# Reordering the first 60 microseconds of a fused spectral filter and max-of-two layer

## The chip, the core and the metric

One core of a Trainium2 chip runs one program. The core has five engines that run independently, each through its own queue of instructions in order: TensorE (PE in the profile, with its weight loads as PEld), VectorE (DVE), ScalarE (ACT), GpSimd (POOL) and SyncE (SP, which here only issues DMAs). An instruction waits for the semaphores of what it needs, and everything behind it on the same queue waits too. The metric is the device time of one execution in microseconds (us); lower is better. The kernel before takes 503.54 us (median of 3 runs, 503.17 to 504.83).

## What is computed

The input x has 8 batches of 3072 positions and 256 channels. Each batch is transformed with a real FFT along the positions, multiplied by a complex filter, and transformed back. The result goes through a small layer with two hidden products of width 1024 whose larger value is kept, and an output product.

```python
X = np.fft.rfft(x, axis=1)
F = (filt_r + 1j * filt_i)[None, :, :]
y = np.fft.irfft(X * F, n=x.shape[1], axis=1)
x = y.reshape(B * S, D)
g = np.maximum(x @ w1, x @ w2)
out = g @ w_out
```

## The kernel before

The FFT of length 3072 = 96 x 32 is done as matrix products in stages, in bf16: a 96-point transform (f1 for batch 1, s1 for later batches, L317 to L356), a trip through DRAM that regroups the result (written from `at` to `ad`, read back as `bt`, f1_read at L334 and s1_read at L358), a 32-point transform (s2, L371), the product with the filter, the inverse 32-point transform (s3, L392), another trip through DRAM (zd to zr, z_read), and the inverse 96-point transform s4 (L422), which leaves a tile of 384 positions in `yt`, channels on the partitions.

The layer uses max(a, b) = relu(a - b) + b. So the kernel holds Wd = w1 - w2, the output weights Wo, and M = w2 Wo, and computes out = relu(y Wd) Wo + y M. Wd is formed on POOL by `prep_wd` (L290), from the f32 copies of w1 and w2 in the buffer WS, which SP's DMAs fill (load_w, L279). w2 is cast to bf16 by DVE in four pieces (`cast_w2`, L284), turned by PE and copied by ACT in two halves (`prep_t`, L294), and multiplied with Wo (`prep_m`, L302). Wo itself comes in by one DMA on POOL's queue, with a cast from f32 (`load_wo`, L287).

The work of the layer is cut into 64 tiles of 384 positions, eight for each batch. Tile tt takes eight steps j of the main loop (L693 to L709). In step j, `moe_h` (L442) makes one 128-wide slice of the hidden products of tile tt (two matmuls, `ph`) and lets DVE or ACT apply the relu; `moe_o` (L463) makes three or four of the 30 matmuls (`po`) that give the output of tile tt - 1: three blocks c of 128 positions, each a sum of eight products with Wo and two with M. Two blocks share one PSUM tile, which DVE copies to `ot` before two DMAs on POOL's queue write it out. In tile 0 the two products with M come last in each block.

The order on every engine is the order of the calls: nothing is rescheduled. `plan(b, step, fn, ...)` (L656) hangs other work behind a step; a batch has 64 steps. In batch 0 these are the rest of `t2` (batch 0's last regrouping), the casts and `prep_t` and `prep_m`, batch 1's f1 in 16 pieces c (plan_f1, L659: each piece one PE matmul and one copy, on ACT for even c and on DVE for odd c; after each odd c SP writes the pair to `ad`), and then f1_read, which issues two DMAs that fill bt for batch 1, 12 columns u each. `plan_f2` (L666) hangs the visits of batch 1 (s2, product, s3, and s1 for batch 2) into fixed steps, the first at step 24, and on SP's queue the loads `load_xf` of batch 2's x (four DMAs for each of the first three pieces, L90 to L98), folded on POOL by `fold` (L100).

Ahead of the main loop stands the opening, which loads x and the filter, makes the tables, and takes batch 0 through its transform. POOL ends it with products of the filter (L382 and L389), then the loads of batch 1's x (`load_x(1, c, 2)`, L88: two of its eight chunks each; chunk k feeds f1 pieces 2k and 2k + 1), prep_wd, load_wo and the table CT. `spin` (L556) issues matmuls whose results nobody uses.

DMA issues carry a lane as well: each of the two families of queues (SP's, POOL's) reuses eight semaphores in turn, so that a DMA also waits until the one eight places before it has landed.

Of the kernel before, what the change touches and what calls it, by code (L numbers as in the profile page):

```python
# [8 lines left out]
FP32 = mybir.dt.float32  # L9
# [6 lines left out]
D = 256  # L16
# [10 lines left out]
def kernel(  # L27
# [15 lines left out]
    V, S, G, TE = nc.vector, nc.scalar, nc.gpsimd, nc.tensor  # L43
# [25 lines left out]
    pso = ctx.enter_context(tc.tile_pool(name="pso", bufs=2, space=bass.MemoryType.PSUM))  # L69
# [8 lines left out]
    def x_tile(b, c):  # L78
        if c % 2 == 0:
            xb[b] = xpool.tile([128, 8, D], BF16, tag="xb", name="xb")  # L80
        return xb[b][:, 4 * (c % 2):4 * (c % 2) + 4]

    def load_x(b, c, n):
        for k in range(c, c + n):
            xb[b, k] = x_tile(b, k)[0:NP]
        src = x[b].rearrange("(p m) d -> p m d", m=NM)
        m0 = 4 * (c % 2)
        G.dma_start(out=xb[b][0:NP, m0:m0 + 4 * n], in_=src[:, 4 * c:4 * c + 4 * n, :])  # L88
# [98 lines left out]
    def table_ct():  # L187
        G.memset(CT, 0.0)
        for g in range(2):
            G.tensor_copy(CT[64 * g:64 * g + 48, :, 0:48].rearrange("p s (u r) -> p s u r", r=2),  # L190
                          C1[0:48].rearrange("p (u s r) -> p s u r", s=2, r=2))
# [92 lines left out]
    def cast_w2(h, c):  # L284
        V.tensor_copy(w2b[:, c, 512 * h:512 * h + 512], w2f[:, c, 512 * h:512 * h + 512])

    def load_wo():  # L287
        G.dma_start(out=Wo, in_=moe_w_out.rearrange("(c p) j -> p c j", p=128))

    def prep_wd(h, engine):  # L290
        js = slice(512 * h, 512 * h + 512)
        engine.tensor_tensor(Wd[:, :, js], w1f[:, :, js], w2f[:, :, js], OP.subtract)  # L292

    def prep_t(jp):  # L294
# [127 lines left out]
    def s4(tt):  # L422
        b, i = divmod(tt, 8)
        y_ = ypool.tile([128, 2, 384], BF16, tag="yt", name="y_")
        for dc in range(2):
            py = ps.tile([128, 4, NP], FP32, tag="ps", name="py")
            for m in range(4):
                TE.matmul(py[:, m], zr[b][:, 4 * i + m, 128 * dc:128 * dc + 128], G1, start=True, stop=True)  # L428
            o_ = y_[:, dc].rearrange("p (t m) -> p t m", m=4)
            i_ = py.rearrange("p m t -> p t m")  # L430
            if dc == 0:
                S.activation(o_, i_, AF.Copy, scale=1.0 / 1536.0)
            else:
                V.tensor_scalar(o_, i_, 1.0 / 1536.0, None, OP.mult)
        yt[tt] = y_
# [18 lines left out]
    po = {}  # L454
    ot = {}

    def out_block(tt, c):
        b, i = divmod(tt, 8)
        dst = out[b * N:(b + 1) * N].rearrange("(c p i m) d -> c i p (m d)", c=3, p=32, i=8)[c, i]
        E = G if tt < 8 * B - 2 else nc.sync  # L460
        E.dma_start(out=dst, in_=ot[tt // 2][:, 3 * (tt % 2) + c])  # L461

    def moe_o(tt, k0, k1):  # L463
        y_, g_ = yt[tt], gt[tt]
        for k in range(k0, k1):
            c, e = divmod(k, 10)
            n = (e + 2) % 10 if tt == 0 else e
            q = 3 * tt + c
            blk = slice(128 * c, 128 * c + 128)
            if e == 0 and (q % 2 == 0 or q == 24 * B - 1):  # L470
                po[0] = pso.tile([128, 2, D], FP32, tag="po", name="po")
            p_ = po[0][:, q % 2]
            if n < 2:
                TE.matmul(p_, y_[:, n, blk], M[:, n], start=(e == 0), stop=(e == 9))  # L474
            else:
                TE.matmul(p_, g_[:, n - 2, blk], Wo[:, n - 2], start=(e == 0), stop=(e == 9))  # L476
            if e == 9 and q >= 24 * B - 2:
                e = q % 6
                if q % 2 == 0:
                    S.activation(ot[tt // 2][:, e], p_, AF.Copy)  # L480
                else:
                    V.tensor_copy(ot[tt // 2][:, e], p_)
                out_block(tt, c)
            elif e == 9 and q % 2 == 1:
                if q % 6 == 1:
                    ot[tt // 2] = opool.tile([128, 6, D], FP32, tag="ot", name="ot")
                e = q % 6
                V.tensor_copy(ot[tt // 2][:, e - 1:e + 1], po[0])  # L488
                for qq in (q - 1, q):
                    out_block(qq // 3, qq % 3)  # L490

# [26 lines left out]
    def s3t(v, pq):  # L518
        pool, tag = (ps, "ps") if v % 2 else (pso, "po")
        pz = [pool.tile([128, 2, 2, 2, 2, NM], FP32, tag=tag, name="pt%d" % g) for g in range(2)]  # L520
        for _ in range(2 if v == 1 else 1):
            TE.matmul(pz[0].rearrange("p i s r c m -> p (i s r c m)"), W1[:, 0:128], W1, start=True, stop=True)
        for i in range(2):
            for s in range(2):
                for dc in range(2):
                    for q, tab in enumerate((VP, VQ)):
                        for g in range(2):
                            TE.matmul(pz[g][:, i, s, :, dc], pq[s][64 * g:64 * g + 64, q, i, 128 * dc:128 * dc + 128],  # L528
                                      tab[64 * g:64 * g + 64, 2 * v + i, s].rearrange("p (r m) -> p r m", r=2),
                                      start=(q == 0), stop=(q == 1))  # L530
        zv = zT.rearrange("p c m (w g) q -> p w g (c m) q", g=2)
        for g in range(2):
            o_ = zv[:, 2 * v:2 * v + 2, g]
            i_ = pz[g].rearrange("p i s r c m -> p i (c m) (s r)")
            if v >= 4 and g == 1:
                V.tensor_copy(o_, i_)
            else:
                S.activation(o_, i_, AF.Copy)

    def t2(c, engines):  # L540
        if c == 0:
            zr[0] = zrpool.tile([96, NM, D], BF16, tag="zr", name="zr")
        n = 4 // len(engines)
        for k, engine in enumerate(engines):
            pr = ps.tile([96, n, D], BF16, tag="ps", name="pr")
            m0 = 4 * c + n * k
            for m in range(n):
                for dc in range(2):
                    TE.transpose(pr[:, m, 128 * dc:128 * dc + 128], zT[:, dc, m0 + m].rearrange("p u q -> p (u q)"),  # L549
                                 I128)  # L550
            if engine is V:
                V.tensor_copy(zr[0][:, m0:m0 + n], pr)  # L552
            else:
                S.activation(zr[0][:, m0:m0 + n], pr, AF.Copy)

    def spin(n):  # L556
        for _ in range(n):
            pd = ps.tile([128, 512], FP32, tag="ps", name="pd")
            TE.matmul(pd, W1[:, 0:128], W1, start=True, stop=True)  # L559
# [70 lines left out]
        pqs[v] = products(v)  # L630
    for v in (4, 5):
        s3t(v, pqs[v])
    for c in (2, 4):
        load_x(1, c, 2)
    prep_wd(0, G)
    load_wo()
    load_x(1, 6, 2)
    prep_wd(1, G)
    table_ct()
    setup.close()  # L640
    apool = ctx.enter_context(tc.tile_pool(name="apool", bufs=3))
# [4 lines left out]
    f1(1, 0, S)  # L646
    spin(1)
    t2(0, (V, S))
    spin(2)
    s4(0)  # L650
    spin(2)


# [2 lines left out]
    def plan(b, step, fn, *a):  # L656
        todo.setdefault((b + step // 64, step % 64), []).append((fn, a))

    def plan_f1(b, nb, steps, read):  # L659
        for c, n in zip(range(1, 16), steps):  # L660
            plan(b, n, f1, nb, c, S if c % 2 == 0 else V)
        plan(b, read, f1_read, nb)
# [12 lines left out]
            plan(b, steps[-1] + (6 if b else 11), s1_read, b + 2)  # L675

    plan(0, 2, t2, 1, (V,))
    for h in range(2):
        for c in range(2):
            plan(0, 3 + 2 * h + c, cast_w2, h, c)  # L680
    plan(0, 5, prep_t, 0)
    plan(0, 7, prep_t, 1)
    plan(0, 8, prep_m)
    for c in range(2, 8):
        plan(0, 8 * (c - 2) + 8, t2, c, (V,))
    plan_f1(0, 1, (0, 1, 1, 3, 4, 4, 5, 6, 6, 7, 8, 10, 11, 11, 12), 13)
    plan_f2(0, (24, 28, 31, 35, 38, 42, 46), ((0,), (1,), (2,), (3,), (4,), (5,), (6, 7)),
            (6, 10, 14, 18, 21, 25, 29, 33), (14, 18, 21, 25, 28, 32, 36, 40))
    for b in range(1, B - 1):
        plan_f2(b, (7, 14, 18, 24, 31, 38, 42) if b > 1 else (14, 18, 24, 30, 34, 39, 42), ((0, 1), (2,), (3,), (4,), (5,), (6,), (7,)),  # L690
                range(-32, 32, 8) if b > 1 else range(-25, 31, 7), range(-22, 42, 8) if b > 1 else range(-15, 41, 7))
# [1 line left out]
    for tt in range(8 * B + 1):  # L693
        b, i = divmod(tt, 8)
        k = 0
        for j in range(8):
# [5 lines left out]
            if tt > 0:  # L702
                n = 3 if j in (3, 7) else 4
# [36 lines left out]
```

## Time and profile before

The profiled execution of the kernel before took 503.8 us, of which 502.0 us lie between its first and last instruction.

| what | value |
|---|---|
| median of 3 runs | 503.54 us (503.17 to 504.83) |
| profiled execution, its span | 503.8 us, 502.0 us |
| PE busy | 488.4 us (97%) |
| DVE, ACT, POOL busy | 331.9, 308.3, 257.5 us |
| granted TensorE clock, mean | 0.992 |
| DMA traffic | 97.20 MB, 194 GB/s |
| PE idle in us 34 to 46 | 2.04 us of 12 |
| PE idle in us 46 to 56 | 0.18 us of 10 |

Busy is the time in which an engine has at least one instruction in work; matmuls overlap, so a busy PE is not necessarily a full one. "A <- B" in a list of waits means that engine and line A stood idle until B was done. A DMA has a time of issue on its queue and a time to landing, from the issue to the last byte's semaphore.

### The profile page before, as it was taken

The page shows a single profiled execution, that of the slowest core. Times are in us where ns is not written, and L with a number is a line of the kernel's source. Part 1 is how long each engine was busy: PE and PEld are TensorE (multiplying, and loading weights), DVE is VectorE, ACT ScalarE, POOL GpSimd, SP SyncE. Part 2 cuts the span into 40 slices and gives each one's busy share as a digit, 9 for nine tenths or more (in the row PEclk, how much of TensorE's full clock was granted, in tenths as well). Part 3 has the DMA queues.
Part 4 walks back from the last instruction along what each step waited for, and adds up shares of the span by engine and source line. Part 5 has one row for each costly group of instructions (what it writes and reads, how often), then busy time and mean ns, then how long its engine had stood idle before and what let it go on. Part 6 is the DMA issues. An engine that isn't in the chain of part 4 may idle for free.

```text
span 502.0 us, 13079 instructions
## 1 busy us (share of the span) xinstructions
PE 488.4 (97%) x5299; PEld 362.1 (72%) x5303; DVE 331.9 (66%) x518; ACT 308.3 (61%) x629; POOL 257.5 (51%) x338
## 2 busy tenths in 40 slices
PE   8688999999999999999999999999999999999997
PEld 3455777777777777777777777777777777777775
DVE  7876688457865777457765687557765687555553
ACT  6776478647774676557764586647774465544442
POOL 7893569547463864645654855537632221222220
PEclk9989999999999999999999999999999999999999
DMA  7999789995799667986779558896769235411112
GB/s 125 150 252 217 230 229 290 306 274 171 212 268 260 175 204 234 250 229 189 198 244 275 187 177 245 235 239 197 197 181 255 78 111 153 168 65 64 64 64 84
DMA packets 77966, 97.20 MB, mean 194 GB/s; under 512 B 8017, under 2 KB 54354, under 8 KB 77842
## 3 DMA queue, kind: packets, MB, share of 16 engines
q1 hardware_dynamic: 64642, 66.73, 49.6%
q0 software_dynamic: 13264, 29.64, 20.3%
q8 instruction: 41, 0.67, 0.6%
q14 instruction: 19, 0.16, 0.1%
HBM read 53.87 MB, written 47.19 MB: 201 GB/s over the span
## 4 chain that ended last, share of the span: by engine, by line
PE 90%; DMA 5%; POOL 2%; issue 1%; ACT 1%; DVE 0%; SPq 0%; POOLq 0%; DVEq 0%
PE po L476 34%; PE ph L448 33%; PE po L474 8%; PE pz L399 5%; PE py L428 4%; PE pa L349 2%; DMA F<-in_filt_r_dram 2%; PE px L376 2%; DMA Wo<-in_moe_w_out_dram 2%; POOL xb L88 1%; DMA F<-F 1%; PE pr L549 1%; POOL pq L382 0%; PE pt L528 0%; PE pm__1132 L306 0%
## 5 line engine op out<-in xcount | busy, mean ns | idle before, releaser
L476 PE MATMUL po<-Wo,gt 128*128 128x256 bf16 x1536 | 261.0, 273 | 0.2 <-DMA Wo<-in_moe_w_out_dram 0.2
L452 ACT ACTIVATE gt<-ph 128x384 bf16<-128x384 f32 x321 | 157.0, 496 | 147.9 <-PE ph L448 147.3
L461 POOL DMA_DIRECT2D out_dram<-ot x186 | 102.6, 555 | 187.1 <-DVE ot L488 184.4
L476 PEld LDWEIGHTS <-gt 128*128 128x128 bf16 x1536 | 146.6, 98 | 66.1 <-issue 10.3
L450 DVE TENSOR_SCALAR gt<-ph 128x384 bf16<-128x384 f32 x191 | 104.9, 552 | 63.1 <-PE ph L448 59.9
L382 DVE TENSOR_TENSOR pq<-px,F 128x1024 bf16<-128x1024 f32 x91 | 107.0, 1219 | 24.2 <-PE px L376 22.6
L448 PEld LDWEIGHTS <-Wd 128*128 128x128 bf16 x1024 | 96.5, 98 | 12.9 <-POOL Wd L292 1.4
L103 POOL TENSOR_TENSOR xb<-XF 128x512 bf16<-128x512 f32 x48 | 61.2, 1276 | 41.3 <-DMA XF<-in_x_dram 21.2
L488 DVE COPY ot<-po 128x512 f32<-128x512 f32 x95 | 65.1, 685 | 25.3 <-PE po L476 25.0
L104 POOL TENSOR_TENSOR xb<-XF 128x512 bf16<-128x512 f32 x48 | 61.0, 1271 | 0.0
L403 ACT ACTIVATE zt<-pz 128x512 bf16<-128x512 f32 x84 | 45.6, 595 | 11.5 <-PE pz L399 8.4
L353 ACT ACTIVATE at<-pa 128x512 bf16<-128x512 f32 x96 | 51.8, 610 | 1.2 <-PE pa L349 0.8
L428 PE MATMUL py<-G,zr 96*128 96x96 bf16 x512 | 32.7, 206 | 0.2
L428 PEld LDWEIGHTS <-zr 96*128 96x128 bf16 x512 | 29.0, 97 | 2.5 <-DVE zr L552 0.4
L399 PE MATMUL pz<-pq,VP 64*64 64x256 bf16 x336 | 21.9, 281 | 0.0
L376 PE MATMUL px<-bt,U 64*64 64x256 bf16 x384 | 19.8, 278 | 1.2 <-ACT VQ L273 0.7
L399 PE MATMUL pz<-pq,VQ 64*64 64x256 bf16 x336 | 20.9, 269 | 0.0
L349 PE MATMUL pa<-xb,CT 64*64 64x512 bf16 x192 | 19.5, 383 | 0.0
L399 PEld LDWEIGHTS <-VP 64*64 64x64 bf16 x336 | 9.7, 105 | 13.3 <-issue 13.3
L376 PEld LDWEIGHTS <-U 64*64 64x64 bf16 x384 | 10.4, 109 | 3.9 <-issue 3.3
L559 PE MATMUL pd<-W 128*128 128x512 bf16 x30 | 10.5, 462 | 1.7 <-DVE zero L145 1.5
L552 DVE COPY zr<-pr 96x1024 bf16<-96x1024 bf16 (+1 forms) x8 | 5.2, 649 | 8.0 <-PE pr L549 8.0
(429 smaller groups left out, 609.7 us busy)
## 6 DMA issues: line engine op xcount, KB each, us to landing
out_dram<-ot POOLq DMA_DIRECT2D x186, 128.0 KB, 3.3
XF<-in_x_dram SPq DMA_DIRECT2D x96, 192.0 KB, 4.6
ad<-at SPq DMA_DIRECT2D x56, 192.0 KB, 3.3
bt<-ad SPq DMA_DIRECT2D x14, 768.0 KB, 9.1
zd<-zt SPq DMA_DIRECT2D x42, 256.0 KB, 2.7
zr<-zd SPq DMA_DIRECT2D x56, 192.0 KB, 4.8
WS<-in_moe_w_dram SPq DMA_DIRECT2D x4, 512.0 KB, 5.1
xb<-in_x_dram POOLq DMA_DIRECT2D x8, 192.0 KB, 5.8
```

Source lines behind the costliest of these rows:

```text
L103: G.tensor_tensor(t_[:, 0], f[:, 0], f[:, 1], OP.add)
L104: G.tensor_tensor(t_[:, 1], f[:, 0], f[:, 1], OP.subtract)
L353: S.activation(at[:, m0:m0 + 2], pa[g], AF.Copy)
L382: E.tensor_tensor(pq, px.rearrange("p (o i) d -> p o i d", o=1).to_broadcast([128, 2, 2, D]), F[:, :, 2 * v:2 * v + 2, s], OP.mult)
L399: TE.matmul(pz[g][64 * s:64 * s + 64, i], tab[64 * g:64 * g + 64, 2 * v + i, s], pq[s][64 * g:64 * g + 64, q, i], start=(q == 0), stop=(q ...
L428: TE.matmul(py[:, m], zr[b][:, 4 * i + m, 128 * dc:128 * dc + 128], G1, start=True, stop=True)
L448: TE.matmul(ph, Wd[:, dc, 128 * j:128 * j + 128], y_[:, dc], start=(dc == 0), stop=(dc == 1))
L450: V.tensor_scalar(gt[tt][:, j], ph, 0.0, None, OP.max)
L452: S.activation(gt[tt][:, j], ph, AF.Relu)
L461: E.dma_start(out=dst, in_=ot[tt // 2][:, 3 * (tt % 2) + c])
L476: TE.matmul(p_, g_[:, n - 2, blk], Wo[:, n - 2], start=(e == 0), stop=(e == 9))
L488: V.tensor_copy(ot[tt // 2][:, e - 1:e + 1], po[0])
```

## The change

On POOL's queue at the end of the opening, the order is now: load of x chunks 2 and 3, W_out, three quarters of w1 - w2, the loads of x chunks 4 to 7, the last quarter of w1 - w2. Before, it was: x chunks 2 to 5, the first half of w1 - w2, W_out, x chunks 6 and 7, the second half. `prep_wd` takes quarters (256 of the 1024 columns) in place of halves.

On DVE, two of the four casts of w2 move into the opening, around s4(0); the other two hang behind steps 4 and 5 (before: the four behind steps 3 to 6). `prep_t(0)` moves from step 5 to step 3 and `prep_m` from step 8 to step 9.

Tile 0's blocks are done in another order, FIRST: the Wo products of blocks 0 and 2, then the M products of both, then block 1. Blocks 0 and 2 lie in different PSUM tiles, so `po` now holds two.

Batch 1's f1 pieces 8 and up move from steps 6 to 12 to steps 9 to 13, piece 4 from step 3 to 2, piece 6 from 4 to 5 and piece 7 from 5 to 6; f1_read moves from step 13 to 14. The first two loads of batch 2's x move from steps 6 and 10 to steps 10 and 12. Nothing is added or taken out but the split of two POOL instructions into four.

```diff
--- before.py
+++ after.py
@@ -287,8 +287,8 @@
     def load_wo():
         G.dma_start(out=Wo, in_=moe_w_out.rearrange("(c p) j -> p c j", p=128))
 
-    def prep_wd(h, engine):
-        js = slice(512 * h, 512 * h + 512)
+    def prep_wd(q, engine):
+        js = slice(256 * q, 256 * q + 256)
         engine.tensor_tensor(Wd[:, :, js], w1f[:, :, js], w2f[:, :, js], OP.subtract)
 
     def prep_t(jp):
@@ -460,16 +460,20 @@
         E = G if tt < 8 * B - 2 else nc.sync
         E.dma_start(out=dst, in_=ot[tt // 2][:, 3 * (tt % 2) + c])
 
+
+    FIRST = ([(c, e) for c in (0, 2) for e in range(8)] + [(c, e) for c in (0, 2) for e in (8, 9)]
+             + [(1, e) for e in range(10)])
+
     def moe_o(tt, k0, k1):
         y_, g_ = yt[tt], gt[tt]
         for k in range(k0, k1):
-            c, e = divmod(k, 10)
-            n = (e + 2) % 10 if tt == 0 else e
+            c, e = divmod(k, 10) if tt else FIRST[k]
+            n = e if tt else (e + 2) % 10
             q = 3 * tt + c
             blk = slice(128 * c, 128 * c + 128)
             if e == 0 and (q % 2 == 0 or q == 24 * B - 1):
-                po[0] = pso.tile([128, 2, D], FP32, tag="po", name="po")
-            p_ = po[0][:, q % 2]
+                po[q // 2 % 2] = pso.tile([128, 2, D], FP32, tag="po", name="po")
+            p_ = po[q // 2 % 2][:, q % 2]
             if n < 2:
                 TE.matmul(p_, y_[:, n, blk], M[:, n], start=(e == 0), stop=(e == 9))
             else:
@@ -485,7 +489,7 @@
                 if q % 6 == 1:
                     ot[tt // 2] = opool.tile([128, 6, D], FP32, tag="ot", name="ot")
                 e = q % 6
-                V.tensor_copy(ot[tt // 2][:, e - 1:e + 1], po[0])
+                V.tensor_copy(ot[tt // 2][:, e - 1:e + 1], po[q // 2 % 2])
                 for qq in (q - 1, q):
                     out_block(qq // 3, qq % 3)
 
@@ -630,12 +634,13 @@
         pqs[v] = products(v)
     for v in (4, 5):
         s3t(v, pqs[v])
-    for c in (2, 4):
+    load_x(1, 2, 2)
+    load_wo()
+    for q in range(3):
+        prep_wd(q, G)
+    for c in (4, 6):
         load_x(1, c, 2)
-    prep_wd(0, G)
-    load_wo()
-    load_x(1, 6, 2)
-    prep_wd(1, G)
+    prep_wd(3, G)
     table_ct()
     setup.close()
     apool = ctx.enter_context(tc.tile_pool(name="apool", bufs=3))
@@ -646,8 +651,10 @@
     f1(1, 0, S)
     spin(1)
     t2(0, (V, S))
+    cast_w2(0, 0)
     spin(2)
     s4(0)
+    cast_w2(0, 1)
     spin(2)
 
 
@@ -675,17 +682,16 @@
             plan(b, steps[-1] + (6 if b else 11), s1_read, b + 2)
 
     plan(0, 2, t2, 1, (V,))
-    for h in range(2):
-        for c in range(2):
-            plan(0, 3 + 2 * h + c, cast_w2, h, c)
-    plan(0, 5, prep_t, 0)
+    for c in range(2):
+        plan(0, 4 + c, cast_w2, 1, c)
+    plan(0, 3, prep_t, 0)
     plan(0, 7, prep_t, 1)
-    plan(0, 8, prep_m)
+    plan(0, 9, prep_m)
     for c in range(2, 8):
         plan(0, 8 * (c - 2) + 8, t2, c, (V,))
-    plan_f1(0, 1, (0, 1, 1, 3, 4, 4, 5, 6, 6, 7, 8, 10, 11, 11, 12), 13)
+    plan_f1(0, 1, (0, 1, 1, 2, 4, 5, 6, 9, 9, 10, 10, 12, 12, 13, 13), 14)
     plan_f2(0, (24, 28, 31, 35, 38, 42, 46), ((0,), (1,), (2,), (3,), (4,), (5,), (6, 7)),
-            (6, 10, 14, 18, 21, 25, 29, 33), (14, 18, 21, 25, 28, 32, 36, 40))
+            (10, 12, 16, 18, 21, 25, 29, 33), (14, 18, 21, 25, 28, 32, 36, 40))
     for b in range(1, B - 1):
         plan_f2(b, (7, 14, 18, 24, 31, 38, 42) if b > 1 else (14, 18, 24, 30, 34, 39, 42), ((0, 1), (2,), (3,), (4,), (5,), (6,), (7,)),
                 range(-32, 32, 8) if b > 1 else range(-25, 31, 7), range(-22, 42, 8) if b > 1 else range(-15, 41, 7))
```

## The prediction

> **What bounds it now.** I read the page first (busy shares, the chain that ended last), then the table by stages, the waits of PE, and the timelines of POOL, SP and PE from 33 to 64 us.
>
> ```profile
> PE 488.4 (97%) x5299; PEld 362.1 (72%) x5303; DVE 331.9 (66%) x518; ACT 308.3 (61%) x629; POOL 257.5 (51%) x338
> PE 90%; DMA 5%; POOL 2%; issue 1%; ACT 1%; DVE 0%; SPq 0%; POOLq 0%; DVEq 0%
> ```
>
> ```profile
> 34.00:46.00 12.00, 9.96 (x102) 5.95 (x104) 9.24 (x19) 7.43 (x15) 7.80 (x9) 1.00 1.05 193
> 46.00:56.00 10.00, 9.82 (x86) 7.47 (x85) 5.39 (x10) 5.46 (x10) 0.45 (x1) 1.00 0.79 238
> ...
> 100.00:200.00 100.00, 100.00 (x1078) 74.63 (x1076) 69.53 (x100) 65.82 (x135) 58.46 (x70) 1.00 0.81 226
> ```
>
> The second table is by stage: length, then busy us of PE, weight loads, DVE, ACT, POOL, the clock, DMA share, GB/s. From 56 us on PE has no idle time worth naming until about 498, so a microsecond gained or lost before that point reaches the end in full, and nothing later can give it back. What an edit of the opening can gain is PE's idle time from 34 to 47 us: 2.04 us, of which the list of waits names these (us in total, times, longest):
>
> ```profile
> PE pt L299 <- DVE w2b L285: 0.7, 1, 0.7
> PE ph L448 <- POOL Wd L292: 0.7, 1, 0.7
> PE ph L448 <- ACT y__984 L432: 0.2, 1, 0.2
> PE po L476 <- DMA Wo<-in_moe_w_out_dram: 0.2, 1, 0.2
> PEld L376 <- DMA bt<-ad: 0.3, 1, 0.3
> ```
>
> The last line is the one to remember: at 62.90 us, at the first visit of batch 1 (step 24), PE's weight load waits for bt, though PE hides it behind a matmul in flight. PE and batch 1's road through DRAM arrive there together. SP's queue shows that road (issue in us, length of the issue, line, DMA):
>
> ```profile
> 51.18 0.43 SPq L93 DMA_DIRECT2D XF<-in_x_dram  x1
> 51.66 0.46 SPq L97 DMA_DIRECT2D XF<-in_x_dram  x1
> 52.16 0.42 SPq L93 DMA_DIRECT2D XF<-in_x_dram  x1
> 52.62 0.43 SPq L97 DMA_DIRECT2D XF<-in_x_dram  x1
> 53.16 1.41 SPq L332 DMA_DIRECT2D ad<-at  x2
> 56.88 1.22 SPq L338 DMA_DIRECT2D bt<-ad  x2
> ```
>
> The last write to ad goes out at 54.2, the read of bt at 56.88 (2.7 later), and its first half lands 5.8 later, at 62.68.
>
> **The change, part by part.**
>
> POOL. After the products (33.89) come x chunks 2-3 (0.53), now W_out (0.93, so 34.4 to 35.3), then quarters of w1 - w2: a half took 2.36, an equal 128x512 add in the folds (L103) 1.28, so I take 1.25 a quarter. The quarters end at 36.5, 37.8 and 39.0; two loads of x (0.52 each) follow to 40.1, the fourth quarter ends at 41.3. Before, the halves ended at 37.26 and 41.01. Hidden columns 4 and 5, for which PE waited 0.67 until 41.07, are ready at 39.0: gain 0.67. Columns 6 and 7 are wanted at about 42.3: 41.3 is in time by 1. The 0.2 for y__984 stays.
>
> DVE. The two casts in the opening (0.41 each) fit into idle times of 0.97 ahead of L434 and 0.63 behind it; without these they would cost 0.41 each in front of y. WS's halves were loaded with 4.5 to 6.7 to landing from issues at 27.0 to 29.4, so by about 36. The other two casts now end near 43.6, where PE, 1.1 us ahead, wants them at 43.4. Of the 0.70 wait I keep 0.2: gain 0.5 here, with a 0.3 wait for a PSUM slot (ACT's 1.02 copy of the earlier w2T) already inside the 1.1.
>
> W_out. Three f1 matmuls (0.22 each) leave the stretch ahead of its first use, so PE wants it at 46.64 - 0.18 - 1.36 - 0.65 = 44.45. On POOL's queue x chunks 2-3 landed at 39.2 and 4-5 near 41.0, and W_out then took 5.6 more to 46.6. Directly behind chunks 2-3 it lands at 39.2 + 4 to 5.6 = 43.2 to 44.8. Between no wait and 0.35 I take 0.1, so 0.1 of the old 0.18 is gained. The split of `po`, FIRST and the quarter adds have one answer: same matmuls, copies and outputs; the first copy to ot comes ten matmuls later, and POOL, which idled 13.6 us ahead of its first output, hides that. Sum so far: 0.67 + 0.5 + 0.1 and some 0.2 of smaller waits, 1.5 us in PE's favour; PE reaches step 24 at 61.4 instead of 62.9.
>
> x, later. Chunks 4-5 are issued at 39.0 instead of 34.4 and stand behind W_out. The last load (6-7) landed at 49.0 before; the bytes on the queue are the same, so it lands there again, and 4-5 some 2 earlier, near 47. f1 piece 8 wants them at 47.8. Cost 0; if they took the 10.9 us that the last load took, 39.0 + 10.9 = 49.9, it would be 2.1.
>
> ```profile
> Wo<-in_moe_w_out_dram POOLq DMA_DIRECT2D x1, 512.0 KB, 9.4
> xb<-in_x_dram POOLq DMA_DIRECT2D x1, 384.0 KB, 10.9
> ```
>
> f1 and bt. On PE everything up to the end of step 13 is the same work as before, so piece 15, now in step 13, is done at 54.40 - 1.5 = 52.9 against 53.46 before, and its copy at 53.7 against 54.2. But SP has more in front of the last write. The write of pieces 10 and 11 goes out near 50.1; then come, in this order, four loads of XF (1.98 us for four above), the write of 12 and 13 (0.35), four more loads (1.98), and only then the last write: 50.1 + 0.35 + 1.98 + 0.35 + 1.98 = 54.8 against 54.2. By lanes it also waits until the second load of the first group (issued 50.9, 3.2 to landing) is in, at 54.1, so that is hidden. It lands 2.7 later if alone, 3.1 as its neighbour did behind loads; I take 2.9: bt's read at 57.7, its first half at 57.7 + 5.8 = 63.5, PE's first product at 63.7. Before it was 62.9. So the 1.5 us won turn into a wait of 2.3 for bt, and the net is 0.8 lost. Ends: with the copy at 53.7 as the only limit and 2.7 for the write, -0.4; with landings of 4.9 and 4.5 for the first XF group (as in its old place) the last write waits for its lane until 55.4 and lands 3.1 later, which is +1.6.
>
> Behind step 24: bt's second half is wanted at step 35, some 11 us later, and the folds of batch 2 keep a slack of 1.5 us or more (fold 2 ends at 70.4, used at 71.9) and shift with SP's queue by under 1. Cost 0.
>
> **The sum.** Against the profiled execution, 503.8 (502.0 of span and 1.8 around): 503.8 - 1.5 + 2.3 = 504.6. That run lies 0.26 above the median of 503.54, so against the median I forecast 504.3.
>
> [...] TensorE was at half clock from about 22.7 to 29.6 (granted clock 0.68 in 22 to 24, 0.50 to 28, 0.61 to 30), after four microseconds with PE busy for 2.27. Two stretches of 2 us with 1.33 and 1.30 busy, at 40 and 44, kept 1.00. [...] The DMA queues from 37 to 43 us, with packets, MB and share of the 16 engines:
>
> ```profile
> q0 software_dynamic: 964, 0.98, 109.0%
> ...
> q1 hardware_dynamic: 3, 0.01, 0.3%
> ```
>
> q0 is POOL's queue and q1 SP's, on which two writes to ad, issued from 39.1 on, took 8.6 us meanwhile. [...]
>
> **Rivals.**
> *Chunks 4-5 come late (slower).* If they land as the load behind W_out did before, PE stands at f1 piece 8 until 49.9, and every later write moves with it: 504.3 + 2.1 = 506.4. For it: 10.9 us on this queue with W_out ahead. Against: x is then first behind W_out, not second, and most of the queue's backlog is older. It makes the kernel slower by over 0.3% from a landing at about 48.6 on. Chance 0.2; with it, 0.1 that lanes or a slow last write alone bring 505.1 to 505.5.
> *The clock drops in the wait.* 6.8 us at half clock cost up to 3.4: 507.7. For it: the drop at 22.7 in a stretch of many small waits; against: the two stretches above. Chance 0.06.
> *bt is no limit (faster).* If the writes reach ad and bt lands by 61.4, all of the 1.5 stays: 503.54 - 1.5 = 502.0. It needs bt's read at 55.6, 1.3 us before the old one, though the last write has eight loads ahead of it. Chance 0.12; half of it with more than 0.3%.
> *Nothing changes at all* (the two effects cancel, 503.2 to 503.9) is the lower part of my own case.
>
> **Chances.** My case, 503.2 to 505.0, has 0.52, the rivals 0.2, 0.1, 0.06 and 0.12. 0.3% is 1.5 us here, about what a measurement of this kernel can tell from no change. Slower by more: 0.2 + 0.1 + 0.06 and a little of my own case's end, 0.37; faster by more 0.06; within 0.57. The range, 502.9 to 506.4, leaves out most of the case with no limit at bt and the clock's.
>
> **What would show it.** In the profile after: no wait of PE for Wd or w2b above 0.2; W_out landing by 45; PE's first L376 of batch 1 with a wait of some 2.3 us for bt near 61.4, and its start at 63.5 to 64; L338's issue at 57.5 to 58; the last two writes to ad each behind four loads of XF. I am wrong if that wait is absent or under 1 us, if PE stands at L324 for xb, or if the clock dips below 1.00 after 60 us.

## The result, and the profile after

| | before | after |
|---|---|---|
| median of 16 runs each | 504.19 us (503.17 to 506.72) | 507.35 us (505.19 to 510.87) |
| profiled execution, its span | 503.8, 502.0 us | 508.84, 507.1 us |
| granted TensorE clock, mean | 0.992 | 0.989 |

The ratio of after to before is 1.0061 (95% interval 1.0040 to 1.0082): the change makes the kernel slower by 0.6%. I had forecast 504.3 us, "within 0.3%" as the likeliest, and a range up to 506.4, which the median exceeds by 0.95.

The profile page of after gives the busy times and the chain that ended last. In the chain, ACT and DVE now have 3% and 2%, where before they had 1% and 0%, and PE's share is 90% in both:

```profile
PE 490.2 (97%) x5303; PEld 362.6 (72%) x5303; DVE 335.5 (66%) x518; ACT 308.7 (61%) x629; POOL 258.6 (51%) x340
PE 90%; DMA 3%; ACT 3%; DVE 2%; POOL 1%; issue 0%; POOLq 0%; ACTq 0%
```

DVE's busy time rose by 3.6 us though it has the same 518 instructions. The table by stages of after (window, length, busy us of PE, weight loads, DVE, ACT and POOL, the granted clock, DMA share, GB/s) shows part of it in 34 to 46 us:

```profile
34.00:46.00 12.00, 9.47 (x99) 5.68 (x98) 10.82 (x18) 7.27 (x14) 8.43 (x11) 1.00 1.09 198
46.00:56.00 10.00, 10.00 (x89) 7.64 (x87) 5.91 (x11) 5.80 (x11) 0.00 (x0) 1.00 0.54 162
64.00:66.00 2.00, 0.00 (x0) 0.00 (x0) 0.00 (x0) 0.00 (x0) 1.02 (x1) 1.00 1.06 343
66.00:68.00 2.00, 1.63 (x16) 0.83 (x17) 0.95 (x1) 0.52 (x2) 0.00 (x0) 0.58 1.11 351
68.00:70.00 2.00, 2.00 (x15) 1.63 (x14) 2.00 (x4) 0.56 (x2) 0.00 (x0) 0.56 1.13 294
```

In 34 to 46 us PE idles 2.53 us, not less than before (2.04) but more, while DVE is busy 10.82 of 12 us where it was 9.24. From 64 to 66 PE does nothing at all, and in the 4 us behind that the granted clock is 0.58 and 0.56: PE then counts as busy, but its groups from px to po (66.37 to 68.19) take 1.82 us, where casts_act below, at a clock of 1.00, has 1.01 for the same (64.55 to 65.56). Of PE's list of waits in after (us in total, times, longest), these are the ones that belong to the change:

```profile
PE px L376 <- DMA bt<-ad: 3.0, 1, 3.0
...
PE pa L324 <- DVE at L327: 1.5, 1, 1.5
...
PE pt L299 <- DVE w2b L285: 0.2, 1, 0.2
```

The waits for Wd and Wo are gone and the one for w2b is down from 0.7 to 0.2, as meant. In their place stand 3.0 us for bt, of which my prediction had 2.3, and 1.5 us for a copy of f1 on DVE, which it did not have at all. The queue of SP in after (issue, length of the issue, line, DMA) gives the road of bt:

```profile
52.32 0.30 SPq L332 DMA_DIRECT2D ad<-at  x1
...
54.64 0.35 SPq L332 DMA_DIRECT2D ad<-at  x1
...
57.08 0.35 SPq L332 DMA_DIRECT2D ad<-at  x1
60.81 1.28 SPq L338 DMA_DIRECT2D bt<-ad  x2
```

In both gaps left out here stand four loads of XF. The read of bt goes out at 60.81 us, 3.9 later than before, and PE's first product of batch 1 starts at 66.37 instead of 62.90. So 3.47 us were lost by that point. The granted clock is 0.50 from 66.33 to 69.74, 3.41 us in which PE counts as busy for 3.38; I estimate the loss as half of that, 1.7. That is 5.2 together, and the span is 5.1 longer.

The timeline of DVE, POOL and PE in after (start, length, engine, line) explains the wait at L324:

```profile
35.26 3.93 POOL L292 TENSOR_TENSOR Wd<-WS 128x512 bf16<-128x512 f32 x3
36.07 0.78 DVE L285 CAST w2b<-WS 128x512 bf16<-128x512 f32 x1
37.60 3.05 DVE L285 CAST w2b<-WS 128x512 bf16<-128x512 f32 x1
39.15 1.06 POOL L88 DMA_DIRECT2D xb<-in_x_dram  x2
40.21 1.55 POOL L292 TENSOR_TENSOR Wd<-WS 128x512 bf16<-128x512 f32 x1
40.58 0.67 DVE L327 CAST at<-pa 96x512 bf16<-96x512 f32 x1
41.30 0.38 PE L324 MATMUL pa<-xb,C 96*96 96x512 bf16 x1 [1.48 <-DVE at L327]
```

The second cast, 0.41 us of work, takes 3.05. It starts at 37.60 inside POOL's three back-to-back subtractions, stays through them and through the two DMA issues behind them, and ends at 40.65: 0.44 after POOL's last issue ended at 40.21. POOL pays little: of its four subtractions the two that began just before a cast ended took 1.48 and 1.55 us, the other two 1.30 and 1.26. The copy of f1 behind the cast on DVE's queue starts at 40.58, and PE waits 1.48 us for it. This is one execution: where the casts pass differs from one to the next, as xf_back and warm show below.

### The profile page after: what moved, and what is told of

It reads as the page before. It is cut to its first block, busy times and chain, and to the rows that moved or that the text cites. A ratio compares the mean times of both kernels' runs of the same rounds, so it can differ in the third digit from the quotient of the medians.

```text
span 507.1 us, 13085 instructions
## 1 busy us (share of the span) xinstructions
PE 490.2 (97%) x5303; PEld 362.6 (72%) x5303; DVE 335.5 (66%) x518; ACT 308.7 (61%) x629; POOL 258.6 (51%) x340
## 4 chain that ended last, share of the span: by engine, by line
PE 90%; DMA 3%; ACT 3%; DVE 2%; POOL 1%; issue 0%; POOLq 0%; ACTq 0%
PE po L480 33%; PE ph L448 32%; PE po L478 8%; PE pz L399 5%; PE py L428 4%; PE pa L349 2%; PE px L376 2%; DMA xb<-in_x_dram 1%; DMA bt<-ad 1%; DMA ad<-at 1%; DVE w2b L285 1%; PE pt L532 1%; PE pr L553 1%; ACT at L509 0%; PE pt L526 0%
## 5 line engine op out<-in xcount | busy, mean ns | idle before, releaser
L428 PEld LDWEIGHTS <-zr 96*128 96x128 bf16 x512 | 28.9, 97 | 3.1 <-DVE zr L556 1.1
L376 PE MATMUL px<-bt,U 64*64 64x256 bf16 x384 | 20.2, 283 | 4.2 <-DMA bt<-ad 3.0
L349 PE MATMUL pa<-xb,CT 64*64 64x512 bf16 x192 | 19.7, 388 | 0.0
L376 PEld LDWEIGHTS <-U 64*64 64x64 bf16 x384 | 10.4, 109 | 7.0 <-DMA bt<-ad 3.4
L349 PEld LDWEIGHTS <-CT 64*64 64x64 bf16 x192 | 8.7, 106 | 2.2 <-ACT gt L452 1.2
```

## The experiments

Two theories stood against each other at first. *Order on SP*: the loss is bt's lateness, from the XF loads that now lie between the last writes to ad; the casts are a side matter. *Casts*: the loss is DVE's stall beside POOL, which makes f1 and with it everything on the road of bt late. A third question is what the clock adds.

To set the profiles side by side whatever their first 34 us were, I measure the distance from the first hidden product of tile 0 (first `ph`) to the first product of batch 1 (`px` from bt), both as starts in PE's timeline, and take off the wait for bt that lies in it:

| kernel | ph | px | distance | wait for bt | without it | median, ratio to before (95% interval) |
|---|---|---|---|---|---|---|
| before | 37.48 | 62.90 | 25.42 | 0 | 25.42 | |
| after | 37.44 | 66.37 | 28.93 | 3.04 | 25.89 | 507.35, 1.0061 (1.0040 to 1.0082) |
| casts_only | 39.45 | 69.87 | 30.42 | 0 | 30.42 | 508.17, 1.0082 (1.0059 to 1.0106) |
| casts_act | 37.70 | 64.55 | 26.85 | 2.79 | 24.06 | 508.40, 1.0104 (1.0082 to 1.0125) |
| xf_back | 38.07 | 63.06 | 24.99 | 0 | 24.99 | 504.16, 1.0006 (0.9988 to 1.0025) |
| xf_only | 38.27 | 65.82 | 27.55 | 1.75 | 25.80 | 505.56, 1.0026 (1.0012 to 1.0040) |
| casts_back | 38.05 | 65.22 | 27.17 | 2.39 | 24.78 | 507.98, 1.0076 (1.0062 to 1.0090) |
| pool_only | 37.84 | 63.38 | 25.54 | 0.69 | 24.85 | 504.39, 1.0004 (0.9991 to 1.0017) |
| act_xf | 38.06 | 62.75 | 24.69 | 0.97 | 23.72 | 504.61, 1.0013 (0.9993 to 1.0032) |
| early | 37.76 | 61.78 | 24.02 | 0.29 | 23.73 | 504.05, 0.9998 (0.9982 to 1.0015) |
| early_cb | 37.94 | 62.68 | 24.74 | 0 | 24.74 | 503.62, 0.9988 (0.9976 to 1.0000) |
| early_trim | 39.70 | 63.36 | 23.66 | 0 | 23.66 | 503.06, 0.9976 (0.9964 to 0.9988) |

The median of before was 503.89 beside casts_only, casts_act, xf_back and casts_back, 504.20 beside xf_only, act_xf, early and warm, and 504.14 beside the rest.

### The two casts: alone on the old kernel, and taken off DVE

casts_only is the kernel before with nothing but the two casts in the opening:

```diff
     t2(0, (V, S))
+    cast_w2(0, 0)
     spin(2)
     s4(0)
+    cast_w2(0, 1)
     spin(2)
...
-    for h in range(2):
-        for c in range(2):
-            plan(0, 3 + 2 * h + c, cast_w2, h, c)
+    for c in range(2):
+        plan(0, 5 + c, cast_w2, 1, c)
```

> The kernel before, with the first two casts of w2 in the opening on DVE as in the changed kernel, and nothing else. Theory of the lock: the first or the second cast takes 1 to 4 us instead of 0.41 because POOL's halves of w1 - w2 and its DMA issues lie beside it, y or f1's first copies come late, PE loses 1 to 2.5 us before 46 us and bt's read moves by as much: 505 to 506.5 against 504.19. Rival (idle DVE time hides the casts, as the prediction had it): 503.5 to 504.3.

It took 508.17 us, more than the 505 to 506.5 that I expected: by itself this part costs as much as the whole change (the two intervals overlap). Its timeline around the cast:

```profile
38.08 4.57 DVE L285 CAST w2b<-WS 128x512 bf16<-128x512 f32 x1
...
39.87 2.35 POOL L292 TENSOR_TENSOR Wd<-WS 128x1024 bf16<-128x1024 f32 x1
...
43.17 0.48 PE L448 MATMUL ph<-y__985,Wd 128*128 128x384 bf16 x1 [3.40 <-DVE y__985 L434]
```

The cast now lasts 4.57 us and ends at 42.65, 0.43 after POOL's second half of w1 - w2 (to 42.22). It starts inside the first half and lasts through the end of that half (38.47) and the two DMA issues between the halves. PE waits 3.40 us for y behind it, and the clock is 0.64, 0.50, 0.50 and 0.65 in the four stretches of 2 us from 42 on; both lie inside its distance of 30.42. Its bt was no limit (no wait at 69.87), because PE itself came so late.

casts_act is the change with the same two casts on ACT:

```diff
-    cast_w2(0, 0)
+    cast_w2(0, 0, S)
...
-    cast_w2(0, 1)
+    cast_w2(0, 1, S)
```

With S as its third argument, `cast_w2` (whose own lines are left out here) calls `S.activation(..., AF.Copy)` in place of `V.tensor_copy`.

> The changed kernel, with the two casts of w2 in the opening done by ACT in place of DVE. Theory of the lock (a DVE cast from SBUF to SBUF cannot run while POOL's adds and DMA issues follow each other, and everything behind it on DVE waits): no DVE instruction of the opening above 0.8 us, PE's wait of 1.48 us at L324 behind f1's first copy gone, W_out's first use near 44.5 to 45 in place of 46.35, bt's read near 59 in place of 60.8, PE still waiting 2.5 to 3 us for bt: 505.3 to 506 against 507.35. Rival (the DVE queue is late for another reason, such as the late landing of w2): the wait stays and the time is that of the changed kernel.

The wait at L324 is gone, and the distance without the wait for bt falls from 25.89 to 24.06: in this pair of executions the stall of DVE beside POOL had cost PE 1.8 us. Yet the kernel did not get faster (508.40, where I expected 505.3 to 506). PE in casts_act comes earlier and waits 2.79 us for bt, whose read, at 59.21, is only 1.6 earlier; the profiled execution kept its clock and took 506.34, the five others had mean clocks of 0.987 to 0.990 and took 508.00 to 511.33. A further 1.0 us of it lies at the end of the program and is found below. So the casts are a real cost to PE, and taking it away alone does not make the kernel faster.

### The order on SP, undone and done alone

xf_back is the change with the first loads of batch 2's x at their old steps; xf_only is the kernel before with two groups of them between the last writes to ad; casts_back is the change with the casts at their old steps; pool_only undoes both and leaves the order on POOL, the quarters, FIRST and the f1 plan. The change also moves the third group of loads, from step 14 to 16, behind the read of bt; the list of the change leaves that out, and xf_back and pool_only put it back too.

```diff
 # xf_back (against after)
-            (10, 12, 16, 18, 21, 25, 29, 33), (14, 18, 21, 25, 28, 32, 36, 40))
+            (6, 10, 14, 18, 21, 25, 29, 33), (14, 18, 21, 25, 28, 32, 36, 40))
 # xf_only (against before)
-            (6, 10, 14, 18, 21, 25, 29, 33), (14, 18, 21, 25, 28, 32, 36, 40))
+            (10, 11, 14, 18, 21, 25, 29, 33), (14, 18, 21, 25, 28, 32, 36, 40))
 # casts_back (against after; pool_only is this and xf_back)
-    cast_w2(0, 0)
-    cast_w2(0, 1)
...
-    for c in range(2):
-        plan(0, 4 + c, cast_w2, 1, c)
-    plan(0, 3, prep_t, 0)
+    for h in range(2):
+        for c in range(2):
+            plan(0, 3 + 2 * h + c, cast_w2, h, c)
+    plan(0, 5, prep_t, 0)
```

> The changed kernel, with the first two loads of batch 2's x back at steps 6 and 10. Theory of the queue (eight loads stand on SP's queue in front of the last write to ad): the last write goes out at the end of its copy, about 55.7 in place of 57.1, bt's read at 58.4 in place of 60.8, PE's wait for bt 0.6 to 1.2 us in place of 3.0, the clock stays at 1.00 after 60 us: 503.8 to 505 against 507.35. Rival (bt is late because f1's pieces are late): the read is earlier by under 0.5 us and the time is over 506.5.

> The kernel before, with the first two loads of batch 2's x at steps 10 and 11 in place of 6 and 10, so that four of them stand on SP's queue ahead of each of the last two writes to ad; nothing else. Theory of the queue: the last write goes out near 55.5 in place of 54.2, the read of bt at 58.5 to 59 in place of 56.9, PE waits 1.7 to 2.2 us for bt at step 24, and where the clock drops after that 1.7 us more: 505.5 to 508 against 504. Rival (the loads are short beside the writes and hidden): 503.5 to 504.5.

> The changed kernel, with the four casts and prep_t(0) at the steps of the kernel before. Theory of the lock: PE's wait of 1.48 at L324 goes, part of it (up to 0.7) comes back as a wait for w2b at L299; bt's read 0.8 to 1.5 us earlier, PE still waits 2.5 to 3 us for it: 505.5 to 506.5. Rival (the casts cost only their 0.41 us each): no change, 507.3.

> The change without its two casts in the opening and without its later XF loads: W_out second, w1 - w2 in four parts, tile 0's new order of blocks and the f1 plan alone. My theory: the whole loss comes from the two parts taken out, so the rest costs nothing: the last two writes to ad stand behind two XF loads each again and bt is read by 57.8, PE meets no wait for bt over 0.3 us and none for Wd; the wait for w2b stays at 0.5 to 0.7. 503.0 to 504.3 beside a before of 504.2 (the same). Rival: the order on POOL's queue or the f1 plan itself costs: 505 or more, with a wait on PE before 62 us that before did not have.

xf_back takes the whole loss away (504.16, ratio 1.0006, in the range that I expected) though its casts still ran on DVE beside POOL:

```profile
36.71 2.00 DVE L285 CAST w2b<-WS 128x512 bf16<-128x512 f32 x1
...
39.10 1.16 DVE L285 CAST w2b<-WS 128x512 bf16<-128x512 f32 x1
```

In this kernel, and in warm, whose opening is that of after unchanged, PE does not wait at L324 but 0.83 us for y (L434), so the 0.78 and 3.05 us of after are one draw of several. The queue of SP shows what changed in xf_back:

```profile
54.27 1.37 SPq L332 DMA_DIRECT2D ad<-at  x2
57.73 1.93 SPq L338 DMA_DIRECT2D bt<-ad  x2
```

The last two writes go out together, with no loads between them, and bt is read at 57.73 instead of 60.81. xf_only confirms it from the other side: eight loads among the last writes of the old kernel put the read at 60.70 (56.88 before) and give PE a wait of 1.75; it is 0.26% slower, with the mean clock at 0.992 or more in nine of twelve runs. casts_back, with DVE free and the late loads in place, is as slow as after (507.98, where I expected 505.5 to 506.5): its read is at 60.08, PE waits 2.39, and the clock falls to half behind it:

```profile
66.00:68.00 2.00, 2.00 (x15) 1.58 (x14) 2.00 (x3) 0.98 (x2) 0.00 (x0) 0.50 1.12 375
```

pool_only is level with before (504.39), though not by the road that I expected, a wait for bt of at most 0.3. Its wait for Wd is gone, the distance without the wait for bt shrinks by 0.6 us, and 0.69 of waiting for bt takes that back: counted from the first ph, bt is read after 19.7 us, where it was 19.4 before. So the order on SP is the main cause. Of the four kernels with the rest of the change in place, the two with the late loads lose 0.76% (casts_back) and 0.61% (after), and the two without lose 0.04% (pool_only) and 0.06% (xf_back), with the casts in either place. What the casts cost depends on where they fall beside POOL: in casts_only they hold PE for 3.40 us, while xf_back's distance without the wait for bt is 24.99, against 24.85 in pool_only. The rest of the change neither gains nor loses.

### The clock

warm is the change with 14 matmuls that nobody uses ahead of the first visit of batch 1, so that PE is not idle while it waits for bt:

```diff
+            if b == 0 and step == 24:
+                spin(14)
             for fn, a in mid.get((b, step), ()):
                 fn(*a)
```

> The changed kernel, with 14 matmuls of spin (0.216 us each, 3.0 us) on PE ahead of the first visit of batch 1, where it waits 3.04 us for bt. Theory of the clock (the wait costs its own length and then half clock for 3.4 us or more, 1.7 us lost each time): the first product with bt starts at 66.4 to 66.6 as before, the granted clock stays 1.00 after 60 us, and the time falls to 505 to 506 from 507.35. Rival (the clock drop is an accident of the profiled run): no gain, or a loss where the wait would have been under 3 us: 507.3 to 508.

It took 506.11 us, ratio 1.0046 (1.0023 to 1.0069), with a mean clock of 0.992 or 0.993 in eight of ten runs. That is just above the 505 to 506 that I expected, and the interval overlaps that of after. After itself divides the same way. In its six runs with a mean clock of 0.992 or more the median is 506.05, in the ten with 0.986 to 0.990 it is 508.18. Of its loss of 3.2 us on before, 1.9 is there with the clock undisturbed, and the half clock adds some 2 us in more than half of the runs. That the drop sits behind the wait for bt is seen in the profiled execution; for the other runs it is inferred from the mean, which does not say where a drop lies: of 35 runs of before, four have 0.989 or 0.990 as well, and three of these took only 503.15 to 503.52 us.

Which wait is followed by a drop can be read from the traces. Between 20 and 490 us the clock changes at 22.74 and 29.56 us in before and at 21.96, 28.78, 66.33 and 69.74 in after: the distances from one to the next are 6.83, 6.83, 37.55 and 3.41 us, that is 2, 2, 11 and 1 times 3.41. In casts_only and casts_back the half clock of the opening ends where pairs of matmuls shorten from 0.24 to 0.19 or 0.20 us, at about 28.9 and 31.9, and the later drops, at 42.57 and 66.00, lie 4 and 10 times 3.41 behind that. So I cut each execution into stretches of that length; in casts_act and xf_only they are counted on from the shortening at about 28.9 and 31.5, which is an inference. These are the stretches that hold the waits of PE of over 1.7 us from 38 us on:

| kernel | wait of PE, its end | stretches | PE busy in them | clock behind |
|---|---|---|---|---|
| after | 3.04, 66.37 | 62.92 to 66.33 | 0.41 | 0.50 for 3.41 us |
| casts_only | 3.40, 43.17 | 39.15 to 42.57 | 0.62 | 0.50 for 6.83 us |
| casts_back | 2.39, 65.22 | 62.59 to 66.00 | 1.02 | 0.50 for 3.41 us |
| casts_act | 2.79, 64.55 | 59.63 to 63.04, 63.04 to 66.45 | 2.13, 1.90 | 1.00 |
| xf_only | 1.75, 65.82 | 62.18 to 65.60 | 1.89 | 1.00 |

Every drop in the table starts at the end of a stretch in which PE was busy for 1.02 us or less. The wait of casts_act is longer than that of casts_back, but an edge cuts it in two, and no drop follows. The edges lie elsewhere in each execution, so a wait of one length may be followed by a drop in one run and not in the next; that is an inference from these five, one execution of each kernel. Busy time does not explain it all: in the opening the clock fell behind a stretch with PE busy for 1.45 us in before (19.32 to 22.74) and for 1.99 in after (18.54 to 21.96).

### Taking the good parts: an early read, and a surprise at the end

act_xf joins casts_act and xf_back. early goes further: it has f1's last pieces two steps sooner, the read of bt at step 12, and the loads of XF at steps 6 and 8.

```diff
 # early (against act_xf)
-    plan_f1(0, 1, (0, 1, 1, 2, 4, 5, 6, 9, 9, 10, 10, 12, 12, 13, 13), 14)
+    plan_f1(0, 1, (0, 1, 1, 2, 4, 5, 6, 8, 8, 9, 9, 10, 10, 11, 11), 12)
...
-            (6, 10, 14, 18, 21, 25, 29, 33), (14, 18, 21, 25, 28, 32, 36, 40))
+            (6, 8, 14, 18, 21, 25, 29, 33), (14, 18, 21, 25, 28, 32, 36, 40))
```

> The changed kernel with both causes undone: the casts of the opening on ACT, the first two loads of batch 2's x at steps 6 and 10. Theory: no wait at L324, L434 or for bt above 0.5 us other than what is left of bt, PE at its first product with bt at 61.8 to 62.5: 502.8 to 503.7 against 504 before. Rival (chunks 4 to 7 of x, loaded later, hold f1 and with it bt): bt's read not before 57, 504 or more.

> The changed kernel with the casts of the opening on ACT, f1's pieces 8 to 15 at steps 8 to 11 in place of 9 to 13, bt's read at step 12, and the first two loads of batch 2's x at steps 6 and 8. Theory: bt's read goes out by 55.5, no wait for bt, and the 1.5 us that PE gains before 46 us reach the end: 502 to 502.8. Rival (f1 then waits for chunks 4 to 7 of x, which landed at 45.2 and 46.9 in the changed kernel, or the loads of XF at 43 to 46 push those back): PE waits at L328 for xb, 503.5 to 505.

Both missed their times (504.61 and 504.05). act_xf still waits 0.97 us for bt, although its distance without that wait is the 23.7 us of early. early reads bt at 55.34, starts batch 1 at 61.78, 1.1 us ahead of before, and PE has finished 1.1 us ahead at the end too; but its span is only 0.1 shorter. (Chunks 6 and 7 landed at 48.1 in after, not at the 46.9 of this expectation; early waits for neither.) The last copies of before and early on DVE are these:

```profile
498.42 0.42 DVE L482 COPY ot<-po 128x256 f32<-128x256 f32 x1 [1.49 <-PE po L476]
497.30 0.42 DVE L490 COPY ot<-po 128x256 f32<-128x256 f32 x1 [1.49 <-PE po L484]
```

From the end of the last DVE copy (L490 in early) to the end of the span it takes 4.2 us, where before, after, xf_back and warm take 3.2. The three kernels with the casts on ACT so far have 4.1 to 4.2. This is the list of DMA queues for that last stretch of early (packets, MB, share of 16 engines):

```profile
q1 hardware_dynamic: 424, 0.39, 27.0%
q14 instruction: 1, 0.01, 0.5%
```

In that stretch there is one more packet, on a queue that carries instructions. The casts give ACT 631 instructions instead of 629. early_trim is early with two of ACT's activations given to DVE, and early_cb is early with the casts back at their old steps on DVE:

```diff
 # early_trim (against early)
+    on_v |= {(5, 3), (5, 7)}
 # early_cb (against early): as casts_back
```

> The kernel early (casts on ACT, XF at steps 6 and 8, f1 read at step 12) with two of ACT's activations at L456 (tile 5) given to DVE, so that ACT's instructions are 629 again instead of 631. In the three kernels with the casts on ACT the span ends 4.2 us after the last DVE copy, with one packet of the instruction queue behind the last output, in all others 3.2 us. Theory: the end waits for a further piece of ACT's instructions, and two fewer take it away: 3.2 us from the last copy to the end, and 1.0 us below early's 504.05: 502.7 to 503.4, faster than before by 0.2 to 0.3%. Rival: the packet has nothing to do with the number of ACT's instructions: 4.2 us remain, 503.7 to 504.5.

> As early, but with the two casts on DVE at before's place (steps 3 to 6), not on ACT: ACT has 629 instructions. Theory: 3.2 us of tail; the wait for w2b (0.5 to 0.7) is back and the bt wait is below 0.3: 503.0 to 503.9. Rival as in early_trim: 504 or more.

Both came out as expected. The tail is 3.2 us again in both, and the stretch from the last copy to the end of early_trim has only this queue:

```profile
q1 hardware_dynamic: 425, 0.39, 34.4%
```

early_trim took 503.06 us, 1.0 less than early and 0.24% less than before (ratio 0.9976, 0.9964 to 0.9988). It has the lowest median of this study; the interval of early_cb reaches down to its ratio. early_cb, at 503.62, has the wait for w2b (0.7) back. That the end of the program waits for a further piece of ACT's instructions is inferred from the packet and the count; that the microsecond of tail is there in the three profiles with 631 and gone in the profiles of early_trim and early_cb with 629 is shown.

### A late use of bt

late_trim leaves the loads of XF late, and moves the use of bt instead (casts on ACT, and the same two activations on DVE):

```diff
-    plan_f2(0, (24, 28, 31, 35, 38, 42, 46), ((0,), (1,), (2,), (3,), (4,), (5,), (6, 7)),
+    plan_f2(0, (28, 31, 34, 37, 40, 43, 46), ((0,), (1,), (2,), (3,), (4,), (5,), (6, 7)),
```

> The change with its XF loads late as they are, casts on ACT, two of ACT's activations given to DVE, and the seven visits of batch 1 at steps 28, 31, 34, 37, 40, 43, 46 instead of 24, 28, 31, 35, 38, 42, 46: the late transposed coefficients (bt) are wanted some 8 us later. Theory (what hurts is PE's wait for bt at 63 us and the half clock after it, not bt's lateness as such): no wait for bt, no half clock after 34 us, 502.7 to 504.0, with 3.2 us of tail. Rival (a late bt costs wherever it is used, by the DVE and ACT work behind it): 505 to 507, with new waits of PE after 70 us.

No wait for bt is left, and still it took 505.86 us (ratio 1.0036, 1.0020 to 1.0053). The waits of PE from 46 to 110 us are now these:

```profile
PE ph L454 <- DVE pq L386: 0.6, 1, 0.6
PE pr L559 <- ACT zt L407: 0.4, 1, 0.4
PE py L432 <- DVE pq L386: 0.2, 1, 0.2
```

They lie between 82 and 88 us: visits three steps apart crowd the products with the filter on DVE and the copies on ACT, and PE waits 1.2 us for those. The mean clock was 0.986 to 0.990 in four of the twelve runs. The rival was right in its time and its new waits: a late bt is paid for at its first use or, where the visits are moved to make room, behind it. No run crowds the visits with an early bt, so how much of this is the crowding alone is open. What else separates 505.86 from before was not traced.

## Why the prediction was wrong

The second half of the mechanism was right: the road of bt, made longer by eight loads of XF in front of the last write, turns into a wait at L376. The first half was not: in after nothing was won ahead of that wait, and the half clock behind it, which the sum put at nothing, came. In the terms of the sum for the profiled execution, 503.8 - 1.5 + 2.3 = 504.6, the gain of 1.5 came out as a loss of 0.4 (PE reaches step 24 at 63.33, not 62.90), the wait of 2.3 as 3.04, and the 1.7 that I estimate for the half clock joins them: 503.8 + 0.4 + 3.0 + 1.7 = 508.9, measured 508.84. casts_back shows that the clock's term was wrong without the casts too: its wait of 2.39 is the one that I forecast, and it took 507.98.

| step of the prediction | forecast | measured |
|---|---|---|
| waits for Wd, w2b, Wo | 0, 0.2, 0.1 | 0, 0.2, 0 |
| W_out lands | 43.2 to 44.8 | 42.7 |
| x chunks 4-5 land | near 47 | 45.2, no wait for them |
| two casts in the opening | no cost | 0.78 and 3.05 us on DVE, 1.48 of waiting on PE |
| PE reaches step 24 | 61.4 | 63.3 |
| last write to ad goes out | 54.8 | 57.08 |
| from there to bt's read | 2.9 | 3.7 |
| bt read | 57.7 | 60.81 |
| PE's wait for bt | 2.3 | 3.04 |
| first product of batch 1 | 63.7 | 66.37 |
| last load of x (chunks 6-7) lands | 49.0 | 48.1 |
| clock after 60 us | 1.00 (0.06 that not) | 0.50 for 3.4 us |

**"The two casts in the opening (0.41 each) fit into idle times of 0.97 ahead of L434 and 0.63 behind it."** This step failed. I priced the cast by the four rows of before, and those ran from 41.09 on, when POOL had finished its subtractions (41.01). I moved it beside POOL's stream without asking what a DVE instruction does there. In after the cast at 37.60 took 3.05 us for 0.41 and stayed through the ends of two subtractions, while POOL barely slowed: its subtraction behind them took 1.55 us, against 1.30 for the same one in casts_act, with the casts on ACT. With the casts on ACT, most of the 1.5 us that I had forecast as PE's gain is there: the distance without the wait for bt is 24.06 in casts_act, against 25.42 before.

**The last write, and "it lands 2.7 later if alone, 3.1 as its neighbour did behind loads; I take 2.9".** The read came 3.1 us later than I had it. Casts on ACT bring the read to 59.21, so 1.6 of it is the casts' doing in these two executions. Of the other 1.5, the write of pieces 10 and 11 left 0.7 later than I took it (50.76 against 50.1 in casts_act) and the last write needed 3.7 us instead of 2.9 until SP could read. The part about the two groups of loads was exact: 4.7 us from that write to the last one, forecast and measured. My upper end for this term, +1.6 net, puts the first product at 64.5, and casts_act has it at 64.55. That is luck in part: I got there by a wait of the last write for its lane, and in casts_act the writes and loads went out back to back.

**The clock's term, nothing behind a wait of 2.3 us.** This step failed too, and with it the chance of 0.06: no run shows the term as a rule, and the runs go both ways. Behind waits of PE of 3.40 (casts_only), 3.04 (after) and 2.39 us (casts_back) the clock fell to 0.50; behind 2.79 (casts_act's profiled execution) and 1.75 (xf_only) it did not. The drop in after lasted 3.41 us. That it matters where the stretches of 3.41 us fall fits the five profiled executions of the table above; that it also makes the two groups of after's runs is argued, not shown. I should have given this rival some 0.4 once a wait of 2.3 us stood in my own sum.

**"The clock drops in the wait ... 507.7"** was thus the rival that came true in the profiled execution and, going by the mean clocks, in more than half of the runs, though its price was too high by itself (an estimated 1.7 us for a drop of 3.41 us, not 3.4): the median reached 507.35 only together with the late bt, and casts_back came to 507.98 without the casts. The rivals of chunks 4-5 (landed at 45.2, wanted at 47.8) and of "bt is no limit" did not occur.

## What to carry to other kernels

A duration holds for the neighbours that it was measured with: before moving a DVE cast between SBUF tensors (0.41 us in its old place, 0.78 to 4.57 beside POOL's subtractions), look at what POOL does in the new place, and if POOL runs back to back there, try the cast on ACT (0.62 us each in casts_act). Where PE arrives at a transfer with no slack, gains ahead of it are worth nothing until the transfer is made earlier (casts_act gained 1.8 us there and took 508.40): bring forward the writes and what stands before them on their queue first. Price a wait of more than 2 us on PE with the half clock that can follow it (0.50 for 3.41 us behind 2.39 and 3.04 us here, none behind 2.79), and look at the tail of the span behind the last copy (3.2 or 4.2 us here) when a gain does not arrive at the end.

## What the runs showed of the hardware

- A DVE cast from SBUF to SBUF that takes 0.41 us behind POOL's subtractions (before, at 41.09) took 0.78 and 3.05 us (after), 4.57 (casts_only), 2.00 and 1.16 (xf_back) beside them. The two longest lasted through the ends of POOL's back-to-back instructions and through the DMA issues among them, and ended 0.44 us after the boundary at 40.21 (after) and 0.43 after the one at 42.22 (casts_only), about the 0.41 us of a cast. The first cast of after ended at 36.85, inside POOL's three subtractions (35.26 to 39.19). Why one boundary and not another was not found. DVE's copy of f1 from PSUM at 40.58 in after, inside POOL's last subtraction, took 0.67 us, against 0.68 at 44.09 with POOL idle.
- In the profiled executions PE's clock fell to 0.50 for 3.41 us behind a wait of 2.39 us (casts_back) and stayed at 1.00 behind one of 2.79 (casts_act). Its changes lie multiples of 3.41 us apart in before, after, casts_only and casts_back. Of the stretches of that length in the table, it fell behind those with PE busy for 0.41, 0.62 and 1.02 us and not behind those with 1.89 us or more; in the opening of after it fell behind one with 1.99.
- With two instructions more on ACT (casts_act, act_xf, early) the time from the last copy to the end was 4.1 to 4.2 us, in the other kernels 3.2; in early one packet (0.01 MB) of the instruction queue lies in it. With two fewer again (early_trim) it was 3.2.
